# Retention attention with a bilinear feed-forward: the first 115 steps in another order, with four casts on other engines

## The chip, the cores and the metric

The kernel runs on one core of a Trainium2 chip. The metric is the time of one execution on the device, in microseconds (us). Engines are named as in the profile: PE (TensorE, matmuls), PEld (its weight loads), DVE (VectorE), ACT (ScalarE), POOL (GpSimd) and SP (SyncE, which issues the DMAs here).

## The reference, cut to what matters

Four batches of eight heads, 768 positions of 64 values each. Each head keeps a 64 x 64 state that decays and takes in an outer product at every position; the output is read from it by the query. The result, 3072 tokens of 512 values, goes through a bilinear feed-forward.

```
gamma = 1.0 - 2.0 ** (-5.0 - arange(H))
for t in range(S):
    state = gamma * state + einsum('bhd,bhe->bhde', k[:, :, t], v[:, :, t])
    y[:, :, t] = 1/sqrt(D) * einsum('bhd,bhde->bhe', q[:, :, t], state)
x = y as (B*S, H*D)                       # 3072 x 512
out = ((x @ w_a) * (x @ w_b)) @ w_out     # 512 -> 1536 -> 512
```

## The kernel before, in words

The positions are cut into slots of 128 (six per batch, 24 in all). Inside a slot the recurrence is done as attention: scores of keys against queries, a causal mask, a product with v, and for what came before the slot a product of the queries with the state. The decay is put into tables by which k and q are scaled. Weights and activations are turned into bf16; sums are float32 in PSUM.

**Written order.** `STEPS_TEXT` (line 39) is a list of steps, and the loop at line 1203 issues them one after the other. Each step issues its instructions on fixed engines, and `seq` (line 171) pins each engine to this order. So an engine does its own steps in the order of the list, whatever the other engines do, and waits by semaphore for the data and buffers that a step needs. A step that waits holds all later steps of its engine. The list is the only thing that sets the order; no planner runs.

**Names of steps in the opening.** The first six slots (batch 0) go as three pairs: pair 0 is slots 0 and 1, pair 1 is slots 2 and 3.

- `P.x.n`: a DMA on SP. `k`, `q`, `v` with a pair's number; `wa.0`, `wa.1`, `wb.0`, `wb.1` are the first and second blocks (256 of 1536 columns, 512 KB) of w_a and w_b (`load_w`, line 229; b's first block goes as two DMAs of 256 KB); `a.1`, `b.1`, `a.2`, `b.2` are the four wide blocks that follow (512 columns each, as two DMAs of 512 KB, line 221); `o.n` are the blocks of w_out. All weight blocks go through six staging buffers in turn (line 132), so the seventh DMA waits until the first buffer has been cast.
- `K.t.e`, `Q.u.r.0.8.e`: scaling of keys (line 403) and queries (line 440) on engine e (D is VectorE, A is ScalarE, G is GpSimd). `v.t.e`: the cast of v (line 450).
- `TK`, `TQ` (line 560): PE transposes the keys or queries of a pair into a PSUM bank, and the engines named copy it out. `TQ.0.1` and `TQ.0.0` are the two halves of pair 0's queries.
- `S2.u.par.where.ee` (line 584): the scores of one slot, two PSUM banks; then per bank the mask. With D VectorE multiplies the bank by the mask (line 602); with A ScalarE first copies the bank to SBUF (line 601), and VectorE masks the copy. The fourth slot is `S2.1.1`.
- `U2` (line 606): the state's update on PE, followed by two casts on ScalarE. `I2` (line 630) and `N2` (line 640 on): queries with the state, masked scores with v. `L2`: the result leaves PSUM as x.
- `Z`: a warm-up product of zeros on PE (line 668 on), of the given widths.
- `tab`: tables for the later batches (line 335), a small product on VectorE and two exponentials on ScalarE.
- `cw`, `cW` (lines 360 and 375): the casts of weight blocks. `cw.a.1.0` casts the first half of a's second block; `cw.b.0.0` casts the first half of the rows of b's first block, `cw.b.0.1` and `cw.b.0.2` the second half of its rows, 128 columns each.
- `A.ft.h`, `G.ft.h`: the products with 128 columns of w_a (line 692) and of w_b (line 708) over half of the first four slots: `h` = 0 is pair 0, 1 is pair 1. `a.J.ft`, `g.J.ft`: the same over all of a group of slots. ScalarE copies a's product out (line 695), and VectorE multiplies the product with b by it (line 710).
- `l`, `C`, `h`, `M` and the others belong to later slots and to the products with w_out; the change moves some of them by a few places.

PSUM has three banks in a ring for the feed-forward (tag `ff`), four for scores and results (`at0`, `at1`, `y0`, `y1`), and one for the state.

Of the kernel before, what the change touches and what calls it, by code (L numbers as in the profile page):

```python
# [36 lines left out]
    (0, 1): ('Z', 'b', 'F'),  # L37
}
STEPS_TEXT = """
P.k.0 P.q.0 P.v.0 P.k.1 P.q.1 P.v.1 P.wa.0 P.wb.0 P.wa.1 P.wb.1 P.a.1 P.b.1 Z.512.512.256 K.1.D K.0.D  # L40
Q.0.0.0.8.D Q.0.1.0.8.D v.0.G v.1.G TK.0.01.A.ff Z.128 TQ.0.1.D.ff TQ.0.0.D.ff Z.256 S2.0.1.at.DD
S2.0.0.ff.DD U2.0.0 Z.512 K.2.G K.3.G Q.1.0.0.8.D Q.1.1.0.8.D v.2.G v.3.G U2.0.1 N2.0.1 I2.0.01
TK.1.01.A.ff N2.0.0 L2.0.AA TQ.1.1+0.DD.ff tab S2.1.0.ff.DD S2.1.1.at.DD U2.1.0 cw.a.0.0.G cw.a.0.1.G
cw.b.0.0.G cw.b.0.1.G cw.b.0.2.G A.0.0 A.1.0 N2.1.0 I2.1.01 N2.1.1 L2.1.AD U2.1.1 G.0.0 G.1.0 P.a.2 P.k.2
P.q.2 P.b.2 P.v.2 P.o.0 P.o.1 P.o.2 P.o.3 P.o.4 P.o.5 l.k.6.S l.q.6.S l.k.7.S l.v.6.S l.v.7.S l.k.8.S
l.q.8.S l.v.8.S cw.a.1.0.G cw.a.1.1.G cw.b.1.0.G cw.b.1.1.G cW.a.1.0.G cW.a.1.2.G cW.a.1.1.G cW.b.1.0.G
cW.b.1.1.G cW.b.1.2.G cW.a.2.0.G cW.a.2.1.G K.5.G A.0.1 G.0.1 A.1.1 K.4.G G.1.1 cW.a.2.2.G cW.b.2.0.G
cW.b.2.1.G cW.b.2.2.G v.5.G v.4.G a.0.2 a.0.3 C.1.G g.0.2 g.0.3 a.0.4 a.0.7 a.0.6 g.0.6 a.0.5 g.0.5 g.0.4
g.0.7 a.0.8 a.0.9 TK.2.01.A.ff Q.2.0.0.8.D Q.2.1.0.8.D a.0.10 TQ.2.01.D.y0 a.0.11 S2.2.0.y.DA
S2.2.1.at.DD g.0.9 g.0.8 U2.2.0 C.0.G N2.2.0 g.0.10 I2.2.01 N2.2.1 L2.2.AD g.0.11 a.1.0 h.0.3.0.3.G C.3.A  # L50
h.0.3.3.6.G C.2.G g.1.0 a.1.1 g.1.1 a.1.6 h.0.2.0.3.D a.1.4 a.1.2 a.1.3 g.1.3 g.1.2 C.4.G C.5.A
# [1184 lines left out]
```

## Time and profile before

| | |
|---|---|
| three runs | 217.09, 217.22, 219.03 us; median 217.22 |
| the profiled execution | 216.89 us, of which the span (first to last instruction) is 215.2 |
| busy: PE, PEld | 208.3 us (97%), 149.2 us (69%) |
| busy: DVE, ACT, POOL | 157.8 (73%), 109.4 (51%), 154.6 (72%) |
| DMA | 39.68 MB, 184 GB/s over the span |
| granted TensorE clock | 1.000 |

How to read it: the page gives the busy time of each engine and the chain of work that ended last. A timeline row is start, length, engine, line, operation, output and input, count, and in brackets the idle time before it with what ended that. A row that says `x2` holds two instructions in a row. A matmul's end is modelled, so that rows of PE overlap by the time of its drain; what a matmul takes of PE is read from the distance of the starts.

### The profile page before, as it was taken

How to read it: one execution, taken by the hardware profiler on the slowest of the kernel's cores; microseconds unless marked ns; L12 is line 12 of the kernel's file. 1: busy time of each engine (PE TensorE's matmuls, PEld its weight loads, DVE VectorE, ACT ScalarE, POOL GpSimd, SP SyncE). 2: the span in 40 equal slices, each digit the busy share in tenths (PEclk: the TensorE clock that was granted, in tenths of full speed). 3: DMA queues.
4: the chain of work that ended last, by engine and by line, in shares of the span. 5: the costliest groups of instructions: out<-in, count | busy, mean ns of one | idle time of the engine just before them, and what ended most of it. 6: DMA issues, size and time to landing. Idle time of an engine off the chain costs nothing.

```text
span 215.2 us, 5685 instructions
## 1 busy us (share of the span) xinstructions
PE 208.3 (97%) x2254; PEld 149.2 (69%) x2254; DVE 157.8 (73%) x289; ACT 109.4 (51%) x243; POOL 154.6 (72%) x178
## 2 busy tenths in 40 slices
PE   7889999999999999999999999999999999999994
PEld 3567445588888888888888776547764444458883
DVE  6886346888965585467588798977788878699852
ACT  3265326375546446445556563654556665751421
POOL 7475869789898798778958999829998976530000
PEclk9999999999999999999999999999999999999999
DMA  5999999999999999999999699940040000000055
GB/s 173 323 332 371 378 359 354 371 230 237 198 225 266 261 200 272 198 229 193 224 202 289 151 189 229 221 101 0 3 165 31 2 3 0 2 0 24 3 195 171
DMA packets 82618, 39.68 MB, mean 184 GB/s; under 512 B 57248, under 2 KB 75552, under 8 KB 82592
## 3 DMA queue, kind: packets, MB, share of 16 engines
q1 hardware_dynamic: 82448, 39.26, 73.2%
q8 instruction: 17, 0.28, 0.6%
q10 hardware_dynamic: 144, 0.07, 0.1%
q14 instruction: 9, 0.07, 0.1%
HBM read 28.31 MB, written 6.29 MB: 161 GB/s over the span
## 4 chain that ended last, share of the span: by engine, by line
PE 92%; DVE 4%; DMA 2%; issue 0%; DVEq 0%
PE a L692 18%; PE g L708 18%; PE mA L811 14%; PE uA L964 10%; PE mB L811 7%; PE uB L964 5%; PE mC L811 4%; PE uC L964 2%; PE y L542 2%; PE at L480 2%; DMA kf<-in_k_dram 2%; PE fA L1064 2%; PE st L502 1%; PE y L529 1%; DVE kq L448 1%; DVE aT L602 1%
## 5 line engine op out<-in xcount | busy, mean ns | idle before, releaser
L710 DVE TENSOR_TENSOR ht<-g,asb 128x256 bf16<-128x256 f32 (+1 forms) x70 | 33.5, 489 | 22.0 <-PE g L708 18.2
L692 PE MATMUL a<-xt,wa_bf 128*128 128x256 bf16 (+1 forms) x280 | 46.5, 300 | 0.0
L708 PE MATMUL g<-xt,wb_bf 128*128 128x256 bf16 (+1 forms) x280 | 46.4, 300 | 0.0
L695 ACT CAST asb<-a 128x256 bf16<-128x256 f32 (+1 forms) x70 | 29.9, 429 | 29.9 <-PE a L692 26.0
L708 PEld LDWEIGHTS <-wb_bf 128*128 128x128 bf16 x280 | 27.1, 98 | 10.0
L692 PEld LDWEIGHTS <-wa_bf 128*128 128x128 bf16 x280 | 26.5, 98 | 10.3 <-DVE xt L358 0.3
L811 PEld LDWEIGHTS <-hs 128*128 128x128 bf16 x282 | 27.3, 98 | 4.1
L971 ACT COPY snap<-uA 128x512 f32<-128x512 f32 x36 | 20.3, 587 | 10.3 <-PE uA L964 7.8
L818 ACT COPY snaps<-mA 128x256 f32<-128x256 f32 x36 | 13.2, 372 | 24.3 <-PE mA L811 22.7
L749 POOL TENSOR_TENSOR hs<-ht,hs 128x384 bf16<-128x384 bf16 (+2 forms) x18 | 19.7, 1099 | 7.3 <-DVE hs L749 4.2
L811 PEld LDWEIGHTS <-ht 128*128 128x128 bf16 x216 | 21.0, 98 | 4.0
L486 DVE TENSOR_TENSOR aT<-at,mask 128x512 bf16<-128x512 f32 x36 | 22.3, 681 | 0.9 <-PE at L480 0.7
L749 POOL TENSOR_TENSOR hs<-ht 128x768 bf16<-128x768 bf16 (+3 forms) x14 | 18.2, 1300 | 4.3 <-DVE ht L710 4.3
L749 POOL TENSOR_TENSOR ht<-gsb,asb 128x512 bf16<-128x512 bf16 x13 | 15.4, 1189 | 7.0 <-DVE gsb L749 7.0
L423 POOL TENSOR_TENSOR kqb<-qf,qtab 128x512 bf16<-128x512 f32 x17 | 19.6, 1162 | 0.8 <-DMA qf<-in_q_dram 0.8
L749 DVE TENSOR_TENSOR osb<-mB,snaps 128x256 f32<-128x256 f32 x24 | 9.9, 421 | 12.2 <-ACT snaps L818 7.2
L811 PE MATMUL mA<-wsum,hs 128*128 128x256 bf16 x144 | 18.5, 273 | 0.0
L423 POOL TENSOR_TENSOR kqb<-kf,ktab 128x512 bf16<-128x512 f32 x14 | 15.5, 1109 | 3.6 <-DMA kf<-in_k_dram 3.3
L555 ACT CAST xt<-y 128x512 bf16<-128x512 f32 x18 | 9.7, 593 | 3.6 <-PE y L529 2.8
L358 POOL CAST vb<-vf 128x512 bf16<-128x512 f32 x13 | 8.1, 646 | 4.3 <-DMA vf<-in_v_dram 4.3
L811 PE MATMUL mA<-wo_bf,ht 128*128 128x256 bf16 x72 | 10.0, 273 | 0.0
L749 DVE TENSOR_TENSOR asb<-uB,snap 128x512 bf16<-128x512 f32 x12 | 8.2, 684 | 2.4 <-PE uB L964 1.7
(157 smaller groups left out, 381.2 us busy)
## 6 DMA issues: line engine op xcount, KB each, us to landing
out_dram<-osb SPq DMA_DIRECT2D x21, 256.0 KB, 2.6
kf<-in_k_dram SPq DMA_DIRECT2D x18, 256.0 KB, 5.2
qf<-in_q_dram SPq DMA_DIRECT2D x9, 512.0 KB, 5.8
vf<-in_v_dram SPq DMA_DIRECT2D x18, 256.0 KB, 5.3
wsta<-in_moe_w_a_dram SPq DMA_DIRECT2D x6, 512.0 KB, 7.7
wsto<-in_moe_w_out_dram SPq DMA_DIRECT2D x6, 512.0 KB, 8.2
wstb<-in_moe_w_b_dram SPq DMA_DIRECT2D x5, 512.0 KB, 8.1
kf<-in_k_dram SPq DMA_DIRECT2D x3, 512.0 KB, 6.7
```

The source lines that it names most:

```text
L423: seq(eng.tensor_tensor(dst, src, tab, op=ALU.mult))
L486: seq(nc.vector.tensor_tensor(aT[t][:, r], at[r], mask.to_broadcast([P, HP, P]), op=ALU.mult))
L555: seq(nc.scalar.copy(xt[key][:, 2 * r : 2 * r + 2, i * P : (i + 2) * P], ys[t // 2][r].rearrange("p j a s n -> p j (a s n)")))
L692: seq(nc.tensor.matmul(a, wa_bf[:, kt, fs], xcols(J, kt, c0, c1), start=(kt == 0), stop=(kt == KT - 1)))
L695: seq(nc.scalar.copy(asb, a))
L708: seq(nc.tensor.matmul(g, wb_bf[:, kt, fs], xcols(J, kt, c0, c1), start=(kt == 0), stop=(kt == KT - 1)))
L710: seq(nc.vector.tensor_tensor(ht[J][:, ft, c0:c1], g, asbs.pop((J, ft, c0)), op=ALU.mult))
L749: seq(eng.tensor_tensor(dst, x, y, op=op))
L811: seq(nc.tensor.matmul(m, w, right[:, j], start=(first and j == 0), stop=(j == NP - 1), skip_group_check=True))
L818: seq(nc.scalar.copy(self.snaps[:, n], self.bank["A"]))
L964: seq(nc.tensor.matmul(m, w, right[:, k], start=(first and k == 0), stop=(k == 1), skip_group_check=True))
L971: seq(nc.scalar.copy(self.snaps[n], self.bank["A"]))
```

## The change

Only the list of steps is edited, from its first step to `g.0.7`: 114 names before and after, the same work. Five steps change their engine: `v.1` from GpSimd to ScalarE, `TQ.0.0` from VectorE to ScalarE, the fourth slot's scores `S2.1.1` leave PSUM by ScalarE (and are then masked by VectorE out of SBUF), `cw.a.1.0` goes from GpSimd to VectorE and `cw.a.1.1` from GpSimd to ScalarE. Among the moved steps:

- SP: the order of the first weight blocks is `wa.0 wa.1 wb.0 wb.1` instead of `wa.0 wb.0 wa.1 wb.1`; `o.1` goes before `o.0`.
- PE: the warm-up `Z.128` follows the first warm-up directly, `Z.256` stands between the two halves of pair 0's query transposes; the first slot's scores come before the second's, and likewise their products with v; `G.1.0` comes before `G.0.0`, `A.1.1` before `A.0.1`, both after these two G; then a.0.3, g.0.3, a.0.2 instead of a.0.2, a.0.3, g.0.2, g.0.3.
- ScalarE and VectorE: `tab` moves from ahead of pair 1's scores to behind `A.1.0`.
- GpSimd: `K.2` before `v.2` as before, `K.4` before `K.5`, `v.4` before `v.5`, and the three steps less that were given away.

```diff
-P.k.0 P.q.0 P.v.0 P.k.1 P.q.1 P.v.1 P.wa.0 P.wb.0 P.wa.1 P.wb.1 P.a.1 P.b.1 Z.512.512.256 K.1.D K.0.D
-Q.0.0.0.8.D Q.0.1.0.8.D v.0.G v.1.G TK.0.01.A.ff Z.128 TQ.0.1.D.ff TQ.0.0.D.ff Z.256 S2.0.1.at.DD
-S2.0.0.ff.DD U2.0.0 Z.512 K.2.G K.3.G Q.1.0.0.8.D Q.1.1.0.8.D v.2.G v.3.G U2.0.1 N2.0.1 I2.0.01
-TK.1.01.A.ff N2.0.0 L2.0.AA TQ.1.1+0.DD.ff tab S2.1.0.ff.DD S2.1.1.at.DD U2.1.0 cw.a.0.0.G cw.a.0.1.G
-cw.b.0.0.G cw.b.0.1.G cw.b.0.2.G A.0.0 A.1.0 N2.1.0 I2.1.01 N2.1.1 L2.1.AD U2.1.1 G.0.0 G.1.0 P.a.2 P.k.2
-P.q.2 P.b.2 P.v.2 P.o.0 P.o.1 P.o.2 P.o.3 P.o.4 P.o.5 l.k.6.S l.q.6.S l.k.7.S l.v.6.S l.v.7.S l.k.8.S
-l.q.8.S l.v.8.S cw.a.1.0.G cw.a.1.1.G cw.b.1.0.G cw.b.1.1.G cW.a.1.0.G cW.a.1.2.G cW.a.1.1.G cW.b.1.0.G
-cW.b.1.1.G cW.b.1.2.G cW.a.2.0.G cW.a.2.1.G K.5.G A.0.1 G.0.1 A.1.1 K.4.G G.1.1 cW.a.2.2.G cW.b.2.0.G
-cW.b.2.1.G cW.b.2.2.G v.5.G v.4.G a.0.2 a.0.3 C.1.G g.0.2 g.0.3 a.0.4 a.0.7 a.0.6 g.0.6 a.0.5 g.0.5 g.0.4
+P.k.0 P.q.0 P.v.0 P.k.1 P.q.1 P.v.1 Z.512.512.256 K.1.D K.0.D P.wa.0 P.wa.1 P.wb.0 P.wb.1 P.a.1 Z.128
+P.b.1 Q.0.0.0.8.D Q.0.1.0.8.D TK.0.01.A.ff TQ.0.0.A.ff Z.256 v.1.A TQ.0.1.D.ff S2.0.0.ff.DD v.0.G K.2.G
+S2.0.1.at.DD U2.0.0 Z.512 K.3.G v.2.G Q.1.0.0.8.D Q.1.1.0.8.D v.3.G U2.0.1 N2.0.0 I2.0.01 N2.0.1
+TK.1.01.A.ff L2.0.AA TQ.1.1+0.DD.ff S2.1.0.ff.DD S2.1.1.at.AA U2.1.0 cw.a.0.0.G cw.a.0.1.G cw.b.0.0.G
+A.0.0 A.1.0 tab cw.b.0.1.G cw.b.0.2.G N2.1.0 I2.1.01 N2.1.1 L2.1.AD P.a.2 U2.1.1 G.1.0 cw.a.1.1.A P.k.2
+P.q.2 P.b.2 P.v.2 G.0.0 P.o.1 P.o.0 P.o.2 P.o.3 P.o.4 P.o.5 l.k.6.S l.q.6.S l.k.7.S l.v.6.S l.v.7.S
+l.k.8.S l.q.8.S l.v.8.S cw.a.1.0.D cw.b.1.0.G cw.b.1.1.G cW.a.1.0.G cW.a.1.2.G cW.a.1.1.G cW.b.1.0.G
+cW.b.1.1.G A.1.1 cW.b.1.2.G cW.a.2.0.G cW.a.2.1.G A.0.1 G.1.1 G.0.1 cW.a.2.2.G K.4.G K.5.G cW.b.2.0.G
+cW.b.2.1.G cW.b.2.2.G v.4.G a.0.3 v.5.G g.0.3 a.0.2 a.0.7 a.0.4 C.1.G g.0.2 a.0.6 g.0.6 a.0.5 g.0.4 g.0.5
```

## The prediction

> **What bounds the kernel now.** I read the page first, for the bound; then the chain of waits over the first 60 us, for what leads up to it; then the timelines of PE, POOL and SP around the place where the chain turns, for what each step there waits on.
>
> ```profile
> span 215.2 us, 5685 instructions
> PE 208.3 (97%) x2254; PEld 149.2 (69%) x2254; DVE 157.8 (73%) x289; ACT 109.4 (51%) x243; POOL 154.6 (72%) x178
> PE 92%; DVE 4%; DMA 2%; issue 0%; DVEq 0%
> ```
>
> PE is the bound and carries 92% of the chain. The change removes no matmul: the four warm-up groups (Z) are the same, and all transposes, scores and products stay. So it can only change the time in which PE stands still, and only in the opening.
>
> ```profile
> 0.80 4.14 DMA kf<-in_k_dram
> ...
> 7.68 0.41 PE tp L576 x4
> ...
> 8.12 0.76 DVE kqT L358 x2
> ...
> 8.93 0.47 PE at L592 x16
> ...
> 9.45 2.48 DVE aT L602 x4
> 11.94 1.44 DVE kq L448 x2
> ...
> 13.86 0.77 DVE kqT L358 x2
> ...
> 18.74 0.98 PE g L708 x8
> ```
>
> The columns are start, length, what. Up to 14.67 us the chain runs through one VectorE sequence: cast the transposed pair 0, mask it (2.48), scale the queries of pair 1 (1.44), cast them (0.77). From 14.67 on PE follows PE. The next view tells how tight that second part is.
>
> ```profile
> 8.14 0.65 PE L674 MATMUL idle<-zero 128*128 128x256 f32 x2
> ...
> 14.67 0.64 PE L592 MATMUL at<-kqT 64*64 64x128 bf16 x32 [0.62 <-DVE kqT L358]
> ...
> 17.44 0.60 PE L651 MATMUL y<-aT,vb 64*64 64x128 bf16 x15
> ...
> 18.25 0.49 PE L623 MATMUL st<-vb,kq 64*64 64x64 bf16 x16
> 18.67 1.05 PE L708 MATMUL g<-xt,wb_bf 128*128 128x256 bf16 x8
> 19.55 0.60 PE L692 MATMUL a<-xt,wa_bf 128*128 128x256 bf16 x4
> ...
> 27.34 1.03 PE L708 MATMUL g<-xt,wb_bf 128*128 128x512 bf16 x4
> ```
>
> ```profile
> 14.77 1.17 POOL L358 CAST wa_bf<-wsta 128x512 bf16<-128x512 f32 x2 [0.33 <-DMA wsta<-in_moe_w_a_dram]
> 15.88 0.61 POOL L358 CAST wb_bf<-wstb 128x512 bf16<-128x512 f32 x1
> 17.88 0.74 POOL L358 CAST wb_bf<-wstb 128x256 bf16<-128x256 f32 x2 [1.38 <-DMA wstb<-in_moe_w_b_dram]
> 19.21 1.17 POOL L358 CAST wa_bf<-wsta 128x512 bf16<-128x512 f32 x2 [0.59 <-DMA wsta<-in_moe_w_a_dram]
> 20.75 1.17 POOL L358 CAST wb_bf<-wstb 128x512 bf16<-128x512 f32 x2 [0.36 <-DMA wstb<-in_moe_w_b_dram]
> ...
> 26.13 1.17 POOL L358 CAST wb_bf<-wstb 128x512 bf16<-128x512 f32 x2 [0.32 <-DMA wstb<-in_moe_w_b_dram]
> ```
>
> The first product with b (G, line 708) starts on PE at 18.67. Its weights are POOL's cast at 17.88, which waited for the DMA and ended at 17.88 + 0.74 = 18.62. So G's weights were ready 0.05 us before PE came for them. The same fit shows at 27.34: that product starts 0.04 us after the casts of 26.13 end (27.30). POOL sits idle before each of these casts until a DMA lands: weights come at the rate of the DMA, and PE is just not late.
>
> ```profile
> 8.47 2.28 SPq L234 DMA_DIRECT2D wstb<-in_moe_w_b_dram  x2
> 10.80 0.55 SPq L234 DMA_DIRECT2D wsta<-in_moe_w_a_dram  x1
> ...
> 15.96 3.05 SPq L226 DMA_DIRECT2D wstb<-in_moe_w_b_dram  x2
> ```
>
> SP issues b's first block (two halves) at 8.47 and a's second block at 10.80, one queue, in this order. They landed by 17.88 and 19.21.
>
> **The change, part by part.** *Second block of a ahead of the first of b.* All four weight blocks are 512 KB. In the new order b.0 holds the third place in the queue, the one that a.1 has now, and the bytes ahead of it are the same. I take the landing of that place as it is: a little before 19.21, say 19.18. POOL's two casts of b's second half then run 19.2 to 19.2 + 0.74 = 19.95. The new order has G.1.0 first, whose last two matmuls need the later of the two casts. Eight of these matmuls take 19.55 - 18.67 = 0.88 us, 0.11 each. G.1.0's first half can run early (its weights are the cast of b's first half), so six are left from 19.97: they end at 20.63, where the next product (A.1.1) starts. That was 19.55: **+1.08 us**. Nothing stands on PE's queue to fill the wait: the products A.1.1 and A.0.1, whose weights a.0 have long been there, are behind G in both orders.
>
> *Does PE come to G later for another reason?* This is covered by the wait as long as PE arrives before 19.97, instead of 18.67.
>
> ```profile
> 6.35 1.28 DVE L448 TENSOR_TENSOR kq<-qf,qtab 128x512 bf16<-128x512 f32 x2
> 10.18 2.04 POOL L423 TENSOR_TENSOR kq<-kf,ktab 128x512 bf16<-128x512 f32 x2 [0.67 <-DMA kf<-in_k_dram]
> 11.86 1.51 DVE L448 TENSOR_TENSOR kq<-qf,qtab 128x512 bf16<-128x512 f32 x2
> 15.65 0.76 ACT L628 CAST gbd<-st 64x256 bf16<-64x256 f32 x2 [0.41 <-PE st L623]
> 20.70 0.43 DVE L710 TENSOR_TENSOR ht<-g,asb 128x256 bf16<-128x256 f32 x1 [0.45 <-PE g L708]
> 36.69 0.59 ACT L601 CAST aT<-at 128x512 bf16<-128x512 f32 x1
> 37.31 0.59 DVE L602 TENSOR_TENSOR aT<-aT,mask 128x512 bf16<-128x512 bf16 x1
> 51.30 1.14 ACT L356 CAST vb<-vf 128x512 bf16<-128x512 f32 x2
> ```
>
> - First pair. The 256-wide warm-up now lies between the two query transposes. Its two passes take about 0.43 us of PE (0.65 less the drain, an estimate), so the second transpose group starts at 7.68 + 0.23 + 0.43 = 8.34, its cast at 8.34 + 0.44 = 8.78. One cast (0.38) instead of two (0.76) remains on VectorE, so scores start at about 9.20 instead of 8.93: +0.27. ScalarE's cast of the other half (0.59, nearest row: the same size out of PSUM) and v.1 (1.14 / 2 = 0.57) follow its copy of the keys; the state update that needs v.1 stands behind the scores.
> - v.1 off POOL is worth nothing there: POOL's next work, K.2 at 10.18, waits for the DMA of k.
> - Masks end at 11.93 + 0.27 = 12.20. The query scaling took 1.51 while POOL was on K.3 until 12.22; the pair of the first block took 1.28. Starting at the end of K.3 it may take 1.28 again, so pair 1 is late by +0.05 to +0.3.
> - The fourth slot's scores: ScalarE copies two banks (2 x 0.59 = 1.2 us) ahead of the state casts (0.76), so those end near 17.3 instead of 16.4; the second half of I2.1, which needs them, comes up at about 17.2. The masks on VectorE cost 0.59 out of SBUF instead of 0.62 a piece, and end between 17.4 and 17.8, as now (14.67 + 0.46 + 2.48 = 17.6). The late tables move behind A.1.0, out of this stretch.
>
> Together PE reaches G between 18.4 and 19.0, I take 18.6. Up to 0.97 us of this can go wrong and cost nothing while b.0 lands at 19.18; with b.0 on time each tenth past 18.67 would cost a tenth.
>
> *What is late next.* The second half of block b.1 now reuses a.1's buffer, and so waits on SP for its two casts, of which VectorE's comes after G.0.0's product: 20.63 + 0.2 + 0.43, plus a cast between 0.38 (bf16 rows) and 0.69 (f32 out of PSUM). I take 0.69, for f32 input: about 21.95, against 19.0 at the latest now (the pair of issues 15.96 + 3.05). Queued behind it on SP are a.2, k, q, b.2 and v. An issue into an empty queue took 4.14 us to land: 21.95 + 4.14 = 26.09, and this block's casts start at 26.13 now. So it is no later, and the product that needs it, now at 27.34, is itself 1.08 later. POOL is relieved of a.1's casts (1.17), which gains nothing where it waits for the DMA. The other orders (g.0.3 before a.0.2, K.4 before K.5, o.1 before o.0) lie on engines and queues with this same slack of 1.08.
>
> Sum: 215.2 + 1.08 = 216.3 span. The profiled execution took 216.89 for a span of 215.2, and the median of three is 0.33 above it: 217.22 + 1.08 = **218.3 us**.
>
> **The rivals.** *b.0 is not late (not slower).* The third place in the queue is late for a reason that need not repeat.
>
> ```profile
> q8 instruction: 1, 0.02, 4.8%
> ```
>
> This is the DMA view from 14.5 to 16 us: one instruction packet that took 4.8% of 16 engines over 1.5 us, 1.15 us of one engine. A landing waits for the slowest engine. Before it, a.0 landed at 14.74; the first half of b.0 was there by 15.88; after it the second half took until 17.85. Places three to five are then 1.4 us apart on average (17.85, 19.18, 20.72). Without the packet the third place would land at 14.74 + 2 x 1.4 = 17.5, casts end at 18.3, and G starts when PE comes: 18.4 to 19.0, that is -0.2 to +0.3, **217.2**. For it: a packet may fall elsewhere. Against: it is fetched as instructions are used up, and nearly the same ones are issued by then. Chance 0.17.
>
> *The queue runs dry (slower still).*
>
> ```profile
> wstb<-in_moe_w_b_dram SPq DMA_DIRECT2D x5, 512.0 KB, 8.1
> ```
>
> The page's list of DMA issues gives 8.1 us from issue to landing for this tile. If b.1's second half takes that from 21.95, it lands at 30.05 instead of 26.1, and PE stops ahead of the product that now starts at 27.34. It decides from 26.1 + 1.1 = 27.2, that is from 5.25 us of landing time; beyond that each microsecond costs one: 217.22 + 1.08 + 0.85 = **219.2** at the middle of the two prices (6.1), 221.1 at 8.1. For it: five transfers stand behind this one wait. Against: the 8.1 us are made by a queue full ahead of it, and what is issued before this block lands by 24.8 now (the block of 26.13 less one place of 1.4). Chance 0.08.
>
> *A second packet* of 1.15 us on the slow engine before 19.2: 217.22 + 1.08 + 1.15 = **219.45**. Chance 0.04.
>
> *PE's clock falls.*
>
> ```profile
> 1.52 4.34 PE L674 MATMUL idle<-zero 128*128 128x512 f32 x6 [1.52 <-DVE zero L263]
> ...
> 10.05 1.12 PE L674 MATMUL idle<-zero 128*128 128x512 f32 x2
> ```
>
> At the start 1280 columns took 4.34 us (3.4 ns each); later 512 took 1.12 (2.2 ns, drain included): PE starts slower. If the new gap, 18.6 to 19.97 with two matmuls in it, brings that back for some 3.4 us of products, they lose half, 1.7: 217.22 + 1.08 + 1.7 = **220.0**. Against: the gap of 0.62 us ahead of 14.67 left the products of 18.67 at 0.11 us per matmul; no row has one of 1.4. Chance 0.05. The Trainium skill ("TensorE: Matmul & The Clock Gate", Part 1) says that the clock drops only after an idle window of about 3.4 us; by that rule this gap is too short and the rival is out. No run here has shown such a drop.
>
> **How the numbers follow.** The forecast has 0.62, with 217.9 to 218.7 as its own range (landing 0.4 us to either side). The rivals have 0.17, 0.08, 0.04 and 0.05; 0.04 is for what I don't see. The range reaches from 217.0 (the lower end of the first rival) to 219.4 (past the middle of the second), and leaves out the clock, the second packet, half of the dry queue and the unseen: 0.17. One per cent, about what a measurement can tell from no change, is 2.2 us. Faster by that, below 215.0, would need nearly all of the opening's gaps: 0.02. Above 219.4 are the clock (0.05), half of the dry queue (0.04), half of the second packet (0.02) and some of the unseen: 0.12. Within: 0.86.
>
> **What would show it.** The profile after should have POOL's two small b casts start near 19.2 (17.88 now) behind a DMA wait, PE idle before L708 for about 1.2 us at 18.6 to 20, and from there the same matmuls 1.1 us later to the end, with no new gap at 28.4. Scores of pair 0 should start near 9.2. I am wrong if b's casts start before 18.3, if PE comes to G after 19.97, or if PE has a gap past 21 us.

## The result and the profile after

The kernel after took 218.86 us (median of 20 runs, 218.11 to 220.31 and one slow execution of 221.41, which the ratio leaves out), the kernel before 217.45 in its own 20 runs. The ratio is 1.0068, 95% interval [1.0047, 1.0089]: slower by 0.5 to 0.9%, within the 1% that the prediction took for about what a measurement can tell from no change. The profiled execution took 219.64 for a span of 217.9; before it was 216.89 and 215.2.

The head of the page of after, and its chain by engine:

```profile
span 217.9 us, 5676 instructions
PE 208.4 (96%) x2244; PEld 148.8 (68%) x2254; DVE 157.8 (72%) x289; ACT 111.8 (51%) x248; POOL 152.4 (70%) x175
PE 85%; SPq 5%; DMA 3%; POOL 3%; issue 2%; DVE 0%; ACT 0%; DVEq 0%; ACTq 0%; POOLq 0%
```

PE works as long as before (208.4, 208.3), so the 2.7 us more of span are time in which it stands. The chain no longer starts with VectorE (4% before, now 0%), but with SP, a DMA and POOL. The chain of waits of after names the place (start, length, what):

```profile
11.83 7.18 DMA wstb<-in_moe_w_b_dram
19.01 0.05 issue
19.07 0.76 POOL wb_bf L358 x2
19.82 0.05 issue
19.87 0.83 PE g L708 x6
20.70 0.87 PE a L692 x8
```

The second half of b's first block lands at 19.01, POOL casts it, and six matmuls of G.1.0 follow. The timeline of PE in after, with the idle time before a row in brackets:

```profile
18.61 0.49 PE L623 MATMUL st<-vb,kq 64*64 64x64 bf16 x16
19.06 0.39 PE L708 MATMUL g<-xt,wb_bf 128*128 128x256 bf16 x2
19.87 0.83 PE L708 MATMUL g<-xt,wb_bf 128*128 128x256 bf16 x6 [0.42 <-POOL wb_bf L358]
20.53 1.04 PE L692 MATMUL a<-xt,wa_bf 128*128 128x256 bf16 x8
...
28.32 1.03 PE L708 MATMUL g<-xt,wb_bf 128*128 128x512 bf16 x4
...
74.55 0.60 PE L692 MATMUL a<-xt,wa_bf 128*128 128x256 bf16 x4 [0.17 <-DVE ht L710]
...
87.13 0.50 PE L811 MATMUL mA<-wsum,hs 128*128 128x256 bf16 x3 [0.84 <-POOL hs L749]
```

A starts at 20.53 (19.55 before), and the product at 28.32 stood at 27.34: +0.98 at both. Then come two stops that before has not: +1.31 from 74 us, +2.31 from 87, and by 184 us some smaller ones have made it +2.75. In this execution the later stops cost more than the opening. POOL's timeline in after shows the first wait, and what goes ahead of the stop at 87:

```profile
18.39 1.42 POOL L358 CAST wb_bf<-wstb 128x512 bf16<-128x512 f32 x3 [2.04 <-DMA wstb<-in_moe_w_b_dram]
...
25.91 1.17 POOL L358 CAST wb_bf<-wstb 128x512 bf16<-128x512 f32 x2 [0.19 <-DMA wstb<-in_moe_w_b_dram]
...
84.12 1.21 POOL L423 TENSOR_TENSOR kqb<-kf,ktab 128x512 bf16<-128x512 f32 x1 [1.64 <-DMA kf<-in_k_dram]
```

`hs` is a sum of blocks of the hidden values, and `wsum`, met below, one of blocks of w_out; VectorE or POOL computes them (line 749), and products with w_out (line 811) read them. POOL computes the `hs` that PE waits for at 87 right behind this scaling of k, and the scaling waited 1.64 us for its load (in before it started at 81.78).

### The profile page after: what moved, and what is told of

The parts are those of the page before. It is cut to its first block, busy times and chain, and to the rows that moved or that the text cites. A ratio compares the mean times of both kernels' runs of the same rounds, so it can differ in the third digit from the quotient of the medians.

```text
span 217.9 us, 5676 instructions
## 1 busy us (share of the span) xinstructions
PE 208.4 (96%) x2244; PEld 148.8 (68%) x2254; DVE 157.8 (72%) x289; ACT 111.8 (51%) x248; POOL 152.4 (70%) x175
## 4 chain that ended last, share of the span: by engine, by line
PE 85%; SPq 5%; DMA 3%; POOL 3%; issue 2%; DVE 0%; ACT 0%; DVEq 0%; ACTq 0%; POOLq 0%
PE g L708 18%; PE a L692 17%; PE mA L811 14%; PE uA L964 9%; PE mB L811 7%; PE uB L964 5%; PE mC L811 3%; DMA wstb<-in_moe_w_b_dram 3%; PE uC L964 2%; PE y L542 2%; PE at L480 2%; SPq L218 2%; SPq L234 2%; POOL hs L749 2%; PE fA L1064 2%
## 5 line engine op out<-in xcount | busy, mean ns | idle before, releaser
L358 POOL CAST vb<-vf 128x512 bf16<-128x512 f32 x12 | 7.6, 651 | 5.1 <-DMA vf<-in_v_dram 5.0
L358 POOL CAST wb_bf<-wstb 128x512 bf16<-128x512 f32 (+2 forms) x11 | 8.0, 749 | 3.9 <-DMA wstb<-in_moe_w_b_dram 3.9
```

The costliest lines, as they stand in the source:

```text
L358: seq(engine.tensor_copy(dst, src))
```

## The experiments

Each run stands beside runs of the kernel before on the same chip. Two questions were open. Which part of the change makes the 1.4 us: the order of the loads alone, as the prediction has it, or the other moves too? And where do the later stops come from: from the late casts of a's second block, from chance, or from PE being late as such? (Where an expectation gives a theory a number, its content stands beside it.)

**Each part alone.** The kernel after with b's first block loaded second again:

```diff
-P.wa.0 P.wa.1 P.wb.0 P.wb.1
+P.wa.0 P.wb.0 P.wa.1 P.wb.1
```

> The kernel after, with the first weight blocks loaded in the old order (a.0, b.0, a.1, b.1); all else as after. Theory one (the place of b.0 in the load queue makes PE wait ahead of G): POOL's two small casts of b.0 start near 18 us (19.07 in the trace of after) and PE has no gap ahead of L708. PE came to G at 19.06 in that trace against 18.67 before, so A.1.1 starts near 19.95: 217.45 + 0.4 = about 217.9 if the stops at 74 and 87 us go as well, about 218.3 if they stay. Theory two (the rest of the change costs it: more work on ScalarE, another order of scores and casts): as after, about 218.9, and PE still starts A.1.1 near 20.5.

Measured: 217.57, ratio 1.0030 [1.0001, 1.0059]. The timeline of PE of this kernel:

```profile
19.28 1.05 PE L708 MATMUL g<-xt,wb_bf 128*128 128x256 bf16 x8
20.16 1.04 PE L692 MATMUL a<-xt,wa_bf 128*128 128x256 bf16 x8
...
86.50 0.50 PE L811 MATMUL mA<-wsum,hs 128*128 128x256 bf16 x3 [0.84 <-POOL hs L749]
```

No stop inside G any more: A is 0.61 late instead of 0.98, all of it from the time at which PE arrives. Of that, up to 0.30 is a wait of VectorE for a load of q at 7 us that the first traces of before and after don't have. The stop at 86.50 stayed.

The kernel before with only the order of the loads changed:

```diff
-P.wa.0 P.wb.0 P.wa.1 P.wb.1
+P.wa.0 P.wa.1 P.wb.0 P.wb.1
```

> The kernel before, with a's second block loaded ahead of b's first, nothing else. Theory one: b.0 takes the third place, its two small casts start near 19.2 us instead of 17.88, PE waits from 18.7 to 19.9 and is 1.0 us late from there: 217.45 + 1.0 = 218.4, up to 218.9 if being late in the load queue also brings stops further on. Theory two: 217.5, no gap ahead of L708.

Measured: 218.08, ratio 1.0050 [1.0019, 1.0080]. Timelines of PE and of POOL:

```profile
19.11 1.37 PE L708 MATMUL g<-xt,wb_bf 128*128 128x256 bf16 x8 [0.39 <-POOL wb_bf L358]
20.32 0.60 PE L692 MATMUL a<-xt,wa_bf 128*128 128x256 bf16 x4
...
61.45 1.47 PE L811 MATMUL mB<-wsum,ht 128*128 128x256 bf16 x12 [0.30 <-DVE osb L749]
```

```profile
18.44 1.50 POOL L358 CAST wb_bf<-wstb 128x512 bf16<-128x512 f32 x3 [2.14 <-DMA wstb<-in_moe_w_b_dram]
```

The order alone makes the wait (A +0.77) and gets a stop later. By the ratios the order alone costs 0.5% and the other moves alone 0.3%, where both together cost 0.68 and, in a second measurement, 0.76%. The intervals are too wide to say whether the two parts add up, and that of the other moves begins at 0.01%. In the traces they don't add: A is 0.77 late by the one, 0.61 by the other and 0.98 by both, since PE can arrive late during the wait for b.0.

**Both kernels again,** unchanged, to see which stops come again.

> The kernel after, unchanged, for a second trace. The gap ahead of L708 (PE goes on at 19.87 us) belongs to the order and should be there again, with PE about 1.0 us later than before at 31 us. The stops at 74 us (0.33) and 87 us (1.0), where POOL waited for the DMA of k: if they are part of the change, they come again near those places; if they are chance, this trace ends about 1.0 to 1.4 us later than before. Time 218.9.

> The kernel before, unchanged, for a second trace. The first trace of it had no gap on PE from 19 us on. If stops such as those at 61, 74 and 87 us of the other traces are chance, one should show here in some place; if they come from PE being late against the loads, this trace has none again. Time 217.1 to 217.4.

Measured: after 218.97, ratio 1.0076 [1.0048, 1.0104]; before 217.75 in its 8 runs, ratio 0.9998 [0.9977, 1.0020]. First PE of after again, then PE of before again:

```profile
19.88 0.83 PE L708 MATMUL g<-xt,wb_bf 128*128 128x256 bf16 x6 [0.49 <-POOL wb_bf L358]
```

```profile
61.31 1.47 PE L811 MATMUL mB<-wsum,ht 128*128 128x256 bf16 x12 [0.28 <-DVE osb L749]
```

The wait in G is there in both traces of after. The later stops are not: this trace of after has none at 74 and 87 (span 216.7), and this trace of before has one at 61 (span 216.2 instead of 215.2). So a stop at 61 needs no change of the kernel, and those at 74 and 87 need not come with it.

The second trace of before also shows how far one trace can be trusted for the slack of b.0: there its casts ended at 17.91 and PE came to G at 18.96, 1.05 us later, where the first trace had 0.05.

**The casts of a's second block.** One explanation of the later stops was that ScalarE and VectorE cast this block late and so hold back its staging buffer and the loads behind it. Both casts went back to GpSimd:

```diff
-cw.a.1.1.A ... cw.a.1.0.D cw.b.1.0.G
+cw.a.1.0.G cw.a.1.1.G cw.b.1.0.G
```

> The kernel after, with both casts of a's second block back on GpSimd as before. In the kernel after these casts sit on ScalarE and VectorE, and a.1's staging buffer is used again only by the fourth load of w_out, so that a.2's second half waits for the cast of another block (issue at 23.0 us against 21.9 before). Here that buffer goes back to a.2's first half. Theory three (late loads behind that wait make POOL late for k, and with it the stops at 74 and 87 us): a.2 issues near 21.1 us, DMA stays full between 23 and 31 us, the stops go: 217.45 + 1.0 = 218.4. Theory four (the stops are chance, or come from PE being late): same as after, 218.9. A gap ahead of L708 in both.

Measured: 219.77 (6 runs), ratio 1.0116 [1.0074, 1.0159]; not faster than after, so the time does not bear the explanation out. The trace does not refute it. From 23 to 31 us the DMA moved 359 GB/s (317 in after, 364 in before), POOL scaled k at 69.56 (71.97 in after), and there is no stop at 74 or 87, as theory three has it. But b.0's casts ended at 20.55 here (19.83 in after), so that A starts at 21.27, and there is a stop of 0.97 us at 63 us; both lengthen the run for other reasons.

Over all twelve traces, the stop at 87 comes in three (after, the first experiment and "The opening as early as before" below), all among the five of kernels that cast this block on ScalarE and VectorE, and in none of the seven with the casts on GpSimd. In these three POOL's scaling of k near 70 us started at 71.8 to 72.0, in the other nine at 68.7 to 69.6. The second trace of after has these casts and 338 GB/s, and no stop; the first experiment has 361 GB/s and the stop. So the late casts stay a possible cause of this stop and are not shown to be one.

**The two products of a ahead of G.** The prediction said that A.1.1 and A.0.1 were ready and only stood behind G:

```diff
-U2.1.1 G.1.0 ... G.0.0 ... A.1.1 ... A.0.1
+U2.1.1 A.1.1 A.0.1 G.1.0 ... G.0.0
```

> The kernel after, with the products A.1.1 and A.0.1 ahead of G.1.0 and G.0.0 on PE, to fill the wait for b.0. My prediction took them to be ready: then they run from 19.06 us, G follows from 19.94, and PE is 0.6 us earlier than in the kernel after: 218.3. The trace of after speaks against it: the x of pair 1, which these two products read, leaves PSUM by ScalarE and VectorE only at 19.4 and 19.58 us. By that they start at 19.6, G at 20.5, and the block ends where it ends now: 218.9.

Measured: 219.07, ratio 1.0070 [1.0049, 1.0091], as after. Its PE timeline:

```profile
18.61 0.49 PE L623 MATMUL st<-vb,kq 64*64 64x64 bf16 x16
19.64 1.05 PE L692 MATMUL a<-xt,wa_bf 128*128 128x256 bf16 x8 [0.54 <-DVE xt L358]
20.52 1.91 PE L708 MATMUL g<-xt,wb_bf 128*128 128x256 bf16 x16
22.27 1.03 PE L692 MATMUL a<-xt,wa_bf 128*128 128x512 bf16 x4
```

PE now waits for VectorE's cast of pair 1's x, ahead of products over pair 1 (`h` = 1). The next block starts at 22.27, in after at 22.28.

**The opening as early as before.** The first experiment's kernel, and the 256-wide warm-up behind both query transposes again:

```diff
-TQ.0.0.A.ff Z.256 v.1.A TQ.0.1.D.ff
+TQ.0.0.A.ff v.1.A TQ.0.1.D.ff Z.256
```

> The kernel after with b.0 loaded in the old place (217.57 us, 0.43 over before), and with the 256-wide warm-up put back behind both query transposes. If the warm-up between the transposes is what holds up the first scores (0.48 us later against the scaling of k than before, of which the next scaling gives back 0.23), PE comes to G 0.25 us earlier: 217.3. If the rest is ScalarE's larger load, no change: 217.6.

Measured: 217.72 (12 runs), ratio 1.0027 [0.9998, 1.0057]. PE reaches G at 18.55, 0.12 earlier than in before, and still no gain shows in the time. This PE timeline has stops further on, although PE was not late at G:

```profile
44.76 1.49 PE L692 MATMUL a<-xt,wa_bf 128*128 128x256 bf16 x12 [0.73 <-ACT asb L695]
...
87.54 0.50 PE L811 MATMUL mA<-wsum,hs 128*128 128x256 bf16 x3 [1.09 <-POOL hs L749]
```

**PE late and nothing else.** If the later stops come from lateness as such, the kernel before must get them too. A warm-up product of 512, 256, or twice 512 columns went in behind A.1.0:

```diff
-cw.b.0.2.G A.0.0 A.1.0 N2.1.0
+cw.b.0.2.G A.0.0 A.1.0 Z.512 N2.1.0
```

> The kernel before with one more 512-wide warm-up product on PE, behind A.1.0: PE is made 0.85 us late at 16.5 us, and no load, no cast and no order is changed. If lateness of PE is paid once, 217.14 + 0.85 = 218.0 and no gap past 20 us. Theory five (PE late against work that the loads pace, GpSimd's above all, makes VectorE and GpSimd meet otherwise and brings stops of their own further on): 218.4 to 218.9, with gaps on PE near 61, 74 or 87 us.

> The kernel before with one warm-up product of 256 columns in front of pair 1's results, so that TensorE is about 0.43 us late from 19 us on and nothing else is changed. The same with 512 columns (0.85 us) cost 1.16 us in the medians. If lateness is passed on as it is: +0.43. If the stops that come on top are in proportion to the lateness (1.16 / 0.85 = 1.37): +0.59. If they are set off as soon as TensorE is a little late, as in the second look at the kernel before, which was 0.3 late and lost 1.07 in all: +0.7 or more, with a stop near 61 us.

> The kernel before with two warm-up products of 512 columns in front of pair 1's results: TensorE about 1.7 us late from 19 us on. If lateness is passed on as it is: +1.7. In proportion (1.37): +2.3. If the stops on top are a fixed amount of 0.3 that any lateness sets off: +2.0. If loads and the other engines, which are ahead by then, take some of the later waits away: less than 1.7.

| warm-up added | PE late by about | median | ratio | stop at 61 to 64 us in its one trace |
|---|---|---|---|---|
| 256 | 0.43 | 218.09 (before 217.27) | 1.0029 [1.0007, 1.0051] | 0.56 |
| 512 | 0.85 | 218.55 (before 217.39) | 1.0057 [1.0032, 1.0081] | 1.01 |
| 512 twice | 1.7 | 219.73 (before 217.27) | 1.0104 [1.0055, 1.0153] | none |

By the ratios the cost is 0.63, 1.24 and 2.26 us, each more than its lateness (by 0.2, 0.4 and 0.6). Each interval, in us 0.15 to 1.11, 0.70 to 1.76 and 1.20 to 3.3, still holds the lateness itself, so the medians point to extra stops and don't prove them; a fixed amount and a proportion can't be told apart. In the traces the product that stood at 27.34 in before is late by 0.53, 0.79 and 1.73. Each trace is a single execution: the one with 512 columns took 219.57, a microsecond over its median, the one with twice 512 took 218.68, a microsecond under. The traces do show the stops, and what the one at 61 hangs on. Here are VectorE and POOL for the half dose, and then for the double one:

```profile
59.36 1.73 DVE L749 TENSOR_TENSOR wsum<-wo_bf,wsum 128x1536 bf16<-128x1536 bf16 x1
```

```profile
55.02 0.70 POOL L358 CAST vb<-vf 128x512 bf16<-128x512 f32 x1 [0.18 <-DMA vf<-in_v_dram]
55.69 2.66 POOL L423 TENSOR_TENSOR kqb<-qf,qtab 128x512 bf16<-128x512 f32 x2
58.32 1.95 POOL L749 TENSOR_TENSOR hs<-ht 128x768 bf16<-128x768 bf16 x1
```

```profile
59.33 1.13 DVE L749 TENSOR_TENSOR wsum<-wo_bf,wsum 128x1536 bf16<-128x1536 bf16 x1
```

```profile
56.00 1.01 POOL L358 CAST vb<-vf 128x512 bf16<-128x512 f32 x1 [1.66 <-DMA vf<-in_v_dram]
56.98 2.67 POOL L423 TENSOR_TENSOR kqb<-qf,qtab 128x512 bf16<-128x512 f32 x2
59.60 2.35 POOL L749 TENSOR_TENSOR hs<-ht 128x768 bf16<-128x768 bf16 x1
```

VectorE comes to `wsum` at the same time, 59.3. With the half dose POOL had begun `hs` at 58.32; `wsum` took 1.73, and PE stopped. With the double dose the load of v came 1 us later, POOL was still on its scaling until 59.65, VectorE went next (1.13), and POOL's `hs` had to wait (2.35 instead of 1.95); PE did not stop. The kernel before is the second case, its VectorE first and then its POOL:

```profile
57.98 1.13 DVE L749 TENSOR_TENSOR wsum<-wo_bf,wsum 128x1536 bf16<-128x1536 bf16 x1
```

```profile
55.05 0.61 POOL L358 CAST vb<-vf 128x512 bf16<-128x512 f32 x1 [0.74 <-DMA vf<-in_v_dram]
55.63 2.67 POOL L423 TENSOR_TENSOR kqb<-qf,qtab 128x512 bf16<-128x512 f32 x2
58.26 2.36 POOL L749 TENSOR_TENSOR hs<-ht 128x768 bf16<-128x768 bf16 x1
```

There VectorE reaches `wsum` 0.32 before POOL's scaling ends (58.30). If PE and with it VectorE is later than that while v's load is on time, POOL's `hs` goes first. All twelve traces of this case go by this order: in the six where POOL's `hs` began first, `wsum` took 1.47 to 1.73 (in two of them it met the POOL instruction after `hs`), and PE stopped in five, but not in the kernel with the two products of a ahead of G; in the six where it came second, `wsum` took 1.13 and PE did not stop at this place. Lateness alone does not decide which: after was 0.98 late and `wsum` went first.

## Why the prediction was right, and where it was not

**The time.** 218.3 was forecast and 218.86 measured, inside the stated range (217.0 to 219.4) and inside 1%, but above the forecast's own 217.9 to 218.7. Of the 0.56 us between them 0.23 is the base (217.22 of three runs, 217.45 of twenty), and 0.33 the cost: 1.41 us instead of 1.08.

**The block b.0 in third place: right, almost to the tenth.** POOL's two small casts were put at 19.2 to 19.95 and ran 19.07 to 19.83. The six matmuls were to start at 19.97 and started at 19.87; A.1.1 was put at 20.63 and came at 20.53 (+0.98 for +1.08). The first and second experiments show that the stop comes from the order of the loads: it goes when the order goes back, and the order alone makes it. The stop itself is 0.6 us and not the 1.2 that the prediction wanted to see there, since PE came later than it took. The slack of 0.05 on which the sum rests was that of one trace (1.05 in the second), so that the agreement to a tenth is in part luck.

**PE's way to G: the size was off.** It was put at 18.4 to 19.0, 18.6 taken; PE came at 19.06. The scores of pair 0 start 9.62 - 5.22 = 4.40 after the key scaling, in before 8.93 - 5.04 = 3.89: +0.51 for the +0.27 forecast. These are PE and then VectorE in after:

```profile
7.90 0.40 PE L576 MATMUL tp<-sort,kq 128*128 128x128 bf16 x4 [0.58 <-DVE kq L448]
8.14 0.65 PE L674 MATMUL idle<-zero 128*128 128x256 f32 x2
8.62 0.39 PE L576 MATMUL tp<-sort,kq 128*128 128x128 bf16 x4
9.62 0.64 PE L592 MATMUL at<-kqT 64*64 64x128 bf16 x32 [0.61 <-DVE kqT L358]
```

```profile
5.22 1.42 DVE L423 TENSOR_TENSOR kq<-kf,ktab 128x512 bf16<-128x512 f32 x2 [0.47 <-DMA kf<-in_k_dram]
...
9.05 0.42 DVE L358 COPY kqT<-tp 128x512 bf16<-128x512 bf16 x1 [1.20 <-PE tp L576]
...
12.55 1.28 DVE L448 TENSOR_TENSOR kq<-qf,qtab 128x512 bf16<-128x512 f32 x2
...
16.80 0.75 DVE L602 TENSOR_TENSOR aT<-aT,mask 128x512 bf16<-128x512 bf16 x2
18.89 0.69 DVE L358 CAST xt<-y 128x512 bf16<-128x512 f32 x1 [1.22 <-PE y L651]
```

The warm-up holds PE for 8.62 - 8.14 = 0.48 (0.43 forecast), and from the end of the copy (9.47) to the scores it is 0.15, where the sum had 0.04; the rest is a later second transpose and a longer copy (0.42 for 0.38). The query scaling of pair 1 gave 0.23 back, as forecast (1.28 for 1.51). The masks out of SBUF take 0.38 each, not 0.59; no wait of PE hangs on them here. The time of arrival also changes from run to run: the unchanged kernel before came to G at 18.67 and at 18.96. In after the lateness lies under the wait for b.0, as the prediction said.

**"Nothing stands on PE's queue to fill the wait: the products A.1.1 and A.0.1, whose weights a.0 have long been there, are behind G": half read.** The weights were there, but these products are over pair 1, whose x VectorE finishes at 18.89 + 0.69 = 19.58. With them in front PE waited for that instead, and ended at the same place (22.27).

**"The second half of block b.1 now reuses a.1's buffer": wrong.** The forecast was an issue at about 21.95, behind the two casts of a's second block (20.11 and 21.07 in after). SP's queue in after:

```profile
19.84 0.37 SPq L226 DMA_DIRECT2D wstb<-in_moe_w_b_dram  x1
21.99 1.92 SPq L226 DMA_DIRECT2D wsta<-in_moe_w_a_dram  x2
```

It went out at 19.84, as b.0's casts ended (19.83). Its casts are the ones at 25.91 (26.13 before), and there is no gap at 28.32, as forecast, but for another reason than the one given.

**"... the same matmuls 1.1 us later to the end": this is the step that failed.** The sum took every matmul after 21 us to be late by the same 1.08, and the other engines to have that much slack; a gap of PE past 21 us was one of the signs of being wrong that the prediction named. After has two, of 0.17 at 74 and 0.84 at 87, and ends 2.7 later in the profiled execution; in the medians the miss is the 0.33 us. Of the twelve traces nine have a gap of at least 0.16 past 21 us, the second one of before among them, so the prediction took for a property of the kernel what was one execution without gaps.

At 61 us the rows show how a stop comes about: POOL, paced by loads, takes its turn ahead of VectorE. The traces with an added warm-up show that a kernel in which only PE is late can get such stops. Lateness is neither enough for stops further on (1.73 late with the double dose, and none) nor needed (0.12 early in the kernel with the warm-up moved back, and stops at 44 and 87). For the stop at 87 us, where PE waits for POOL behind a late load of k, no run shows why that load was late; that, and the sum of the smaller stops behind it, stay open. So does what the other moves cost: 0.3% with an interval from 0.01%, and 0.27% with one from -0.02% once their lateness at G is gone.

**The rivals.** An instruction packet fell into the same stretch again (DMA view of after, 16 to 17.5 us):

```profile
q8 instruction: 1, 0.02, 4.7%
```

So b.0 was late, and "b.0 not late" is out. Its reason, that the packet may fall elsewhere, was not borne out: in each of the twelve traces one packet lies between 15 and 16.5 us, and none from 16.5 to 18. PE did not stop ahead of the product at 28.32, so the dry queue is out as well. The clock stayed: after the stop six matmuls start within 20.53 - 19.87 = 0.66, 0.11 each, as before, and the granted clock is 1.000. This agrees with the Trainium skill ("TensorE: Matmul & The Clock Gate", Part 1), by which the clock falls after an idle window of about 3.4 us.

## What to carry to other kernels

Before a load is moved back in its queue, find the product that needs it and read how much earlier it was ready: here it was 0.05 us in one trace and 1.05 in another, and with the order alone casts that ended 1.3 us later made the next product 0.77 us later. One trace gives one value of such a slack, so take it from several. A product can fill another's wait only if both its operands are there, so read the activation's row as well as the weight's. In a kernel that is bound by one engine, don't count on a delay at the start being handed on unchanged: engines paced by loads keep their times and can take their turns in another order, and the medians here, though not their intervals, put the cost above the delay.

## What the runs showed of the hardware

VectorE's `wsum`, a tensor operation with two inputs from SBUF, did not run side by side with POOL's tensor operations. In all twelve traces it started during one and ended 0.81 to 0.82 us after that one's end: 58.30 to 59.11 in before (57.98 + 1.13), 60.27 to 61.09 with the half dose (58.32 + 1.95, 59.36 + 1.73), 59.65 to 60.46 with the double one. Read so, the recorded 1.13 and 1.73 are a wait and 0.81 of work, and POOL's 2.36 instead of 1.95 is the same wait the other way round. The Trainium skill ("SBUF — State Buffer", "SBUF: two separate sides") says that the two engines share a pair of ports as an exclusive lock, which a VectorE instruction with two inputs from SBUF needs against a GpSimd one that reads SBUF: the one that starts first holds it for its whole instruction. The rows agree.

The third place in the load queue landed at nearly the same time whichever block stood there: in five traces POOL cast a.1 from 18.92 to 19.92 (19.21 in before), and in the five with b.0 there it cast b.0's second half from 19.07 to 19.81 (19.07 in after). One instruction packet of 4.7 to 4.8% of 16 engines over 1.5 us lies in the stretch ahead of it in before and after. That the packet makes the lag was only argued; all traces have it, and no run took it away.
